# Three stages on one core: output tiles in threes, a later preparation, paired column groups and deferred routing

## The chip, the cores and the metric

The kernel runs on one core of a Trainium2 chip. The metric is the device time of one execution in microseconds (us), lower being better. Each time given for a kernel is the median of several runs. One further execution is taken with the hardware profiler; all rows of the trace come from it.

The core has a matrix engine (PE, with its weight loads shown as PEld), a vector engine (DVE), an engine for activations and copies (ACT, also called ScalarE), GpSimd (POOL) and a queue engine (SP) that issues most DMAs.

## What is computed

Three layers follow one another. The input of each is the output of the layer ahead of it.

```python
# attention: 4 batches x 8 heads, 576 positions, head_dim 64, 128 features
proj = q_or_k @ w_phi; proj -= max(abs(proj))
phi  = concat([exp(proj), exp(-proj)])
out  = (phi_q @ (phi_k.T @ v)) / (phi_q @ sum(phi_k) + 1e-6)
# routed experts: 2304 tokens, width 512, 8 experts, hidden width 1024
logits = x @ w_gate + modality_bias[modality_id]
e = argmax(logits);  g = softmax(logits)[e]
x = g * (relu(x @ w1[e]) @ w2[e])
# gated layer: hidden width 1536
out = ((x @ w_a) * (x @ w_b)) @ w_out
```

All inputs and the output are float32.

## The kernel before, in words

Products that have to be exact to about float32 are made of three matmuls (`mm3`, lines 51 to 54): each operand is split into a high and a low part, and high x high, high x low and low x high are added in PSUM. So every operand is first copied to its high part (mostly by ACT) and then has the low part made by a subtraction (mostly by DVE, in the attention partly by POOL).

**Order of the work.** The kernel is written in Tile: instructions are traced in program order, each gets a priority from its place in that order, and a list scheduler then lays down, from estimated durations, one fixed sequence for each engine; an engine runs its sequence strictly in order. `tc.high_priority(offset=-n)` makes what is traced inside it count as if it came n instructions later, so that it gives way to the next n. Only in the gated layer is the sequence of PE written by hand (`manual_schedule`, lines 866 and 870).

**Attention** (class `Attn`, lines 57 to 265) works in eight units of two heads and two batches, in nine rounds r (lines 912 to 921): in round r `a_steps(r)` makes the features of unit r (`phi`, `turn`) and its sums over positions (`kv`), `b_steps(r - 1)` finishes the unit before (`kvx`, lines 210 to 222, then `num`, lines 224 to 265), and `t_steps(r + 1)` splits the inputs of the next. `kvx` multiplies the sums by the gate weights and copies the product from PSUM to SBUF (tile `kx`, line 221, on DVE); `num` needs `kx`. `num` also leaves partial router logits in `lgp`.

**Routing** (class `Route`, lines 350 to 515) turns the logits of one half of the tokens (1152) into expert tiles: four steps, `start` (constants, gate), `rank`, `place` and `table`, each a chain of small DVE instructions with a few small matmuls. The steps of half 0 are put among the attention steps: `start` and `rank` in round 5, `place` in round 6, `table` in round 7 (line 921). Those of half 1 stand in the expert layer, at steps 0, 2, 4 and 6 (`side`, line 948).

**Experts** (class `Moe`, lines 518 to 650) run four tiles of up to 608 tokens, two for each half. A tile has eight steps (`NJ`), so there are 32 in all; k counts them. Steps 0 to 3 of a tile do two hidden blocks each (`l1`, lines 577 to 591), steps 4 to 7 one output block each (`l2`, lines 593 to 601). Both treat the 608 columns as two groups g of 304 (`CG`). In `l1` each group has a PSUM tile of its own out of six (`ps_l`, line 924); ACT takes the relu of it (tile `hh`, line 588) and DVE makes the low part (`hl`, line 589). In `l2` each group has a PSUM tile too, copied to `y` by ACT (line 601). Weights of a step are loaded two steps ahead and split (`splitw`, lines 545 to 552), tokens are gathered by POOL's indirect DMA (`gather`), transposed on PE and split (`transp`, lines 562 to 575, tiles `mxh` and `mxl`).

**Preparation** (`Moe2.prep`, lines 699 to 717, with `narrow`, lines 677 to 697) turns the weights of the gated layer, which come as 64-bit words, into float32, forms the sums that a Strassen-like scheme needs, splits them and stores them to DRAM (`wsc`). There are twelve blocks f; eight (`NPRE`) are prepared during the experts, spread evenly from step K0 = 0 to K1 = 27 of the 32 at a priority 200 lower (lines 951 to 957), four in the gated layer. At step K1 the buffers of the preparation are given back and the first weights and terms of the gated layer are fetched (`open_first`).

**Gated layer** (class `Moe2`, lines 653 to 872) runs 36 stages: three groups p of six output tiles (128 tokens x 512 each), twelve blocks f for each group. A stage makes seven products (`abp`, in two PSUM buffers, copied by ACT to `pc`, line 836), combines them on DVE, and adds the stage's part to the six accumulators of the group with the stage after it (`outp`, lines 802 to 813). After the last block of a group `finish` (lines 784 to 800) scales the six accumulators into SBUF tiles `o`, every other one on ACT (line 793) and DVE (line 791), and POOL scatters each to its rows of the output by an indirect DMA (line 794). The pool of `o` has `OB` = 2 buffers (line 674), so the third `o` waits until the first scatter has landed.

Of the kernel before, what the change touches and what calls it, by code (L numbers as in the profile page):

```python
# [20 lines left out]
P = 128  # L21
# [17 lines left out]
LOWP = 200  # L39
OB = 2  # L40
LOWP2 = 60
# [5 lines left out]
def f32(ap):  # L47
    return ap.bitcast(F32)
# [8 lines left out]
class Attn:  # L57
# [152 lines left out]
    def kvx(self, u, b):  # L210
        nc, st = self.nc, self.u[u]
        hp = u % 4
        ps = self.ps_t.tile([P, 512], F32, tag="t", name="kxp")
        t = st.pop(("kvs", b))
        for h in range(2):
            for c in range(2):
                i = 2 * h + c
                nc.tensor.matmul(ps[:, 73 * i:73 * i + 73], t[:65, 128 * i:128 * i + 128],
                                 self.cst["iw"][:, 2 * hp + h, :], start=True, stop=True)
        x = self.p_kx.tile([P, 4, 73], F32, tag=f"kx{b}", name="kx")  # L220
        nc.vector.tensor_copy(x, ps[:, :292].rearrange("p (i n) -> p i n", i=4))
        st["kx", b] = x
# [295 lines left out]
class Moe:  # L518
# [58 lines left out]
    def l1(self, T, f):  # L577
        nc = self.nc
        wh, wl = T["w", f // 2]
        for g in range(2):  # L580
            gs = slice(g * CG, g * CG + CG)
            ps = self.ps_l.tile([P, 512], F32, tag="l", name="hp")
            for c in range(4):
                i = 4 * (f % 2) + c
                mm3(nc, ps[:, :CG], wh[:, i, :], wl[:, i, :], T["xh"][:, c, gs], T["xl"][:, c, gs], c == 0, c == 3)
            hh = self.p_h.tile([P, CG], F32R, tag=f"h{f}{g}", name="hh")
            hl = self.p_h.tile([P, CG], F32R, tag=f"l{f}{g}", name="hl")
            nc.scalar.activation(hh, ps[:, :CG], AF.Relu)
            nc.vector.scalar_tensor_tensor(out=hl, in0=ps[:, :CG], scalar=0.0, in1=f32(hh), op0=ALU.max,
                                           op1=ALU.subtract)  # L590
            T["h", f, g] = (hh, hl)

    def l2(self, T, m):
        nc = self.nc
        wh, wl = T["w", 4 + m]
        for g in range(2):
            ps = self.ps_l.tile([P, 512], F32, tag="l", name="yp")
            for f in range(8):
                hh, hl = T["h", f, g]
                mm3(nc, ps[:, :CG], wh[:, f, :], wl[:, f, :], hh, hl, f == 0, f == 7)  # L600
            nc.scalar.copy(self.y[T["rt"].bp][:, m, ds(T["s"][g], CG)], ps[:, :CG])

# [50 lines left out]
class Moe2:  # L653
# [13 lines left out]
    def pools(self, ctx, ps_a, ps_l):  # L667
        tc = self.tc
        pool = lambda n, b: ctx.enter_context(tc.tile_pool(name=n, bufs=b, side="right", reuse_waits="tile"))
        self.p_w[1] = pool("f_w1", 1)  # L670
        self.p_t[1] = pool("f_t1", 4)
        self.p_c = pool("f_c", 1)
        self.p_g = pool("f_g", 2)
        self.p_o = pool("f_o", OB)
        self.ps_a, self.ps_l = ps_a, ps_l
# [103 lines left out]
    def run(self, ws, ts, src0, side):  # L779
# [4 lines left out]
        def finish(p):  # L784
            for m, acc in enumerate(accs.pop(p)):
                bp, b = divmod(2 * p + m // 3, HALF // n)
                o = self.p_o.tile([P, DM], F32, tag="o", name="o")
                c = b * (n // P) + m % 3
# [3 lines left out]
                else:  # L792
# [3 lines left out]
                    out_offset=bass.IndirectOffsetOnAxis(ap=self.routes[bp].perm[:, c:c + 1], axis=0),  # L796
                    in_=o[:, :], in_offset=None)
                for other in self.stores:
# [74 lines left out]


def interleave(*lists):
    items = []
    for n, l in enumerate(lists):
        for i, s in enumerate(l):
            items.append(((i + 0.5) / len(l), n, s))
    items.sort(key=lambda a: (a[0], a[1]))  # L880
    for _, _, s in items:
        s()
# [3 lines left out]
def trn_kernel(ctx, tc, qk, v, w_phi, mod_id, w_gate, bias, wm, wf, out):  # L886
# [10 lines left out]
    with ExitStack() as actx:  # L897
# [14 lines left out]
        for r in range(9):  # L912
            if r + 1 < 8:
                at.load(r + 1)
            if r == 2:
                bs = bias_sel(nc, cpool, keep, bias, mod_id)
                routes = [Route(nc, rpool, lgp[i], bs[i], i) for i in range(2)]
                rsteps = routes[0].steps(wkpool, at.ps_t)
            interleave(at.b_steps(r - 1) if r > 0 else [], at.a_steps(r) if r < 8 else [],
                       at.t_steps(r + 1) if r + 1 < 8 else [],  # L920
                       {5: rsteps[0:2], 6: rsteps[2:3], 7: rsteps[3:4]}.get(r, []) if r > 2 else [])
    with ExitStack() as mctx:
        ps_t = mctx.enter_context(tc.tile_pool(name="ps_t", bufs=2, space=PSUM, **tl))
        ps_l = mctx.enter_context(tc.tile_pool(name="ps_l", bufs=6, space=PSUM, **tl))
        ypool = ctx.enter_context(tc.tile_pool(name="y", bufs=1, **tl))
# [21 lines left out]
        rs = routes[1].steps(wk1, ps_t)  # L947
        side = {2 * f: [rs[f]] for f in range(4)}
        side[7] = [close_work]
# [4 lines left out]

        K0, K1 = 0, len(tiles) * mo.NJ - 5
        for f in range(NPRE):
# [27 lines left out]
    ps_l = ctx.enter_context(tc.tile_pool(name="ps_l2", bufs=2, space=PSUM, **tl))  # L984
    m2.pools(ctx, ps_a, ps_l)
    m2.run(ws, ts, src0[0], side)

# [56 lines left out]
```

## Time and profile before

| | us |
|---|---|
| median of 3 runs | 934.85 |
| the runs | 929.9, 934.85, 939.41 |
| the profiled execution | 940.45 |
| its span, first to last instruction | 938.7 |

A row of the timeline gives the start and the length of an instruction in us, what it does (engine, line, operation, output<-inputs, shape), and in brackets how long its engine sat idle before it and what ended the idle time. A window gives busy us of each engine in a stretch, then the TensorE clock that was granted there as a share of its higher level (1.00 is 2.4 GHz, 0.50 is 1.2 GHz; a value between them is a stretch that holds both). A group of lines gives the number of instructions, their busy time together and the mean length of one in ns.

### The profile page before, as it was taken

What the parts mean: (1) busy time and instruction counts of PE and PEld (TensorE: products, weight loads), DVE (VectorE), ACT (ScalarE), POOL (GpSimd) and SP (SyncE); (2) the same over time, 40 slices, a digit from 0 to 9 for tenths busy, and PEclk for the clock granted to TensorE, in tenths of its full rate; (3) what the DMA queues carried; (4) which work ended last, traced back from release to release, by engine and by line L of the source; (5) the groups of instructions that cost most, each with busy time, mean ns of one, the idle gap of its engine ahead of it and who ended that gap; (6) DMA issues with size and microseconds to landing.
All of it is one profiled execution on the core that took longest, in us unless ns stands there. A gap on an engine that the chain in (4) does not pass through costs nothing. (4 is left out here: it accounts for less than half of the span.)

```text
span 938.7 us, 15310 instructions
## 1 busy us (share of the span) xinstructions
PE 880.0 (94%) x5645; PEld 833.4 (89%) x5645; DVE 671.3 (72%) x1252; ACT 438.3 (47%) x806; POOL 187.4 (20%) x171
## 2 busy tenths in 40 slices
PE   6899999899799799999989999978999998999994
PEld 4899998899799799999988989967999998999993
DVE  7878899969799998986239889856454466554552
ACT  5577666555344454554324445444333344333332
POOL 6443333301343543220002111002000001000002
PEclk7999998899899799999989999979999999999998
DMA  7332330112567688795037998586666667766631
GB/s 246 102 104 77 105 105 13 29 57 64 199 203 268 245 287 307 277 322 188 29 131 290 371 317 312 189 305 206 213 202 205 203 201 244 223 203 202 202 124 67
DMA packets 74309, 179.21 MB, mean 191 GB/s; under 512 B 8912, under 2 KB 27808, under 8 KB 74224
## 3 DMA queue, kind: packets, MB, share of 16 engines
q1 hardware_dynamic: 71184, 168.39, 53.3%
q0 software_dynamic: 3040, 9.75, 3.1%
q8 instruction: 46, 0.75, 0.3%
q14 instruction: 39, 0.32, 0.1%
HBM read 140.36 MB, written 37.75 MB: 190 GB/s over the span
## 5 line engine op out<-in xcount | busy, mean ns | idle before, releaser
L836 ACT COPY pc<-abp 128x384 f32<-128x384 f32 x252 | 120.4, 479 | 195.6 <-PE abp L54 193.9
L52 PE MATMUL abp<-yh,fw 128*128 128x384 f32 x504 | 173.6, 344 | 16.1 <-DMA fw<-wsc 6.4
L54 PE MATMUL abp<-yh,fw 128*128 128x384 f32 x504 | 172.6, 342 | 0.2 <-DMA fw<-wsc 0.2
L53 PE MATMUL abp<-yl,fw 128*128 128x384 f32 x504 | 172.4, 342 | 0.0
L52 PEld LDWEIGHTS abp<-yh,fw 128*128 128x128 f32 x504 | 97.0, 192 | 25.9 <-ACT pc L836 7.6
L689 POOL TENSOR_SCALAR cvs<-cvs 128x768 f32<-128x768 f32 x24 | 59.2, 2468 | 250.4 <-ACT cvs L688 244.9
L53 PEld LDWEIGHTS abp<-yl,fw 128*128 128x128 f32 x504 | 97.0, 192 | 7.8
L54 PEld LDWEIGHTS abp<-yh,fw 128*128 128x128 f32 x504 | 96.7, 192 | 0.7 <-DMA fw<-wsc 0.7
L54 PE MATMUL op<-fw,gl 128*128 128x512 f32 x216 | 85.9, 398 | 1.3 <-DVE gl L826 1.3
L52 PE MATMUL op<-fw,gh 128*128 128x512 f32 x216 | 86.1, 398 | 1.0 <-ACT gh L825 1.0
L53 PE MATMUL op<-fw,gh 128*128 128x512 f32 x216 | 85.4, 395 | 0.0
L794 POOL DMA_INDIRECT out<-o,perm x18 | 17.7, 983 | 318.5 <-ACT o L793 311.7
L53 PE MATMUL hp<-mxl,wh 128*128 128x304 f32 x256 | 79.1, 310 | 1.5 <-DVE mxl L575 1.5
L52 PE MATMUL hp<-mxh,wh 128*128 128x304 f32 x256 | 79.5, 314 | 0.6 <-ACT mxh L574 0.6
L54 PE MATMUL hp<-mxh,wl 128*128 128x304 f32 x256 | 78.7, 308 | 0.0
L53 PE MATMUL yp<-hl,wh 128*128 128x304 f32 x256 | 77.3, 303 | 0.0
L52 PE MATMUL yp<-hh,wh 128*128 128x304 f32 x256 | 77.0, 303 | 0.0
L54 PE MATMUL yp<-hh,wl 128*128 128x304 f32 x256 | 77.0, 302 | 0.0
L236 PE MATMUL nmp<-kx,qts 128*128 128x73 f32 (+1 forms) x640 | 73.3, 271 | 1.8 <-DVE grest L478 1.8
L236 PEld LDWEIGHTS nmp<-kx,qts 128*128 128x128 f32 (+1 forms) x640 | 69.7, 187 | 4.0 <-issue 3.0
L185 ACT ACTIVATE qts<-qtp 128x512 f32<-128x512 f32 (+1 forms) x80 | 40.2, 552 | 47.0 <-PE qtp L182 46.8
L127 POOL TENSOR_TENSOR xtl<-qk,xth 128x512 fp32r<-128x512 f32 (+1 forms) x35 | 44.3, 1268 | 88.0 <-ACT xth L126 83.0
(201 smaller groups left out, 2052.9 us busy)
## 6 DMA issues: line engine op xcount, KB each, us to landing
fw<-wsc SPq DMA_DIRECT2D x72, 512.0 KB
fw<-wsc SPq DMA_DIRECT2D x144, 256.0 KB
raw<-in_moe_w SPq DMA_DIRECT2D x24, 768.0 KB
s<-in_moe_w SPq DMA_DIRECT2D x32, 512.0 KB
fw<-wsc SPq DMA_DIRECT2D x72, 128.0 KB
wsc<-whi SPq DMA_DIRECT2D x12, 640.0 KB
wsc<-wsum SPq DMA_DIRECT2D x12, 640.0 KB
wsc<-whi SPq DMA_DIRECT2D x12, 512.0 KB
```

The costliest lines, as they stand in the source:

```text
L52: nc.tensor.matmul(out, lh, rh, start=start, stop=False)
L53: nc.tensor.matmul(out, lh, rl, start=False, stop=False)
L54: nc.tensor.matmul(out, ll, rh, start=False, stop=stop)
L127: (nc.vector if u == 0 else nc.gpsimd).tensor_sub(lo[:, x:y], src, f32(hi[:, x:y]))
L185: nc.scalar.activation(t[:, s, :n, :], ps[:, :n, :], AF.Exp, scale=1.0 - 2.0 * s)
L236: nc.tensor.matmul(ps[pp, o, :], qt[:, c, a, pp], st["kx", b][:, 2 * h + c, :], start=c == 0, stop=c == 1)
L689: nc.gpsimd.tensor_scalar(out=s.bitcast(F32), in0=s.bitcast(F32), scalar1=LEAST, scalar2=None, op0=ALU.max)
L794: st = nc.gpsimd.indirect_dma_start(out=self.out[:, :], out_offset=bass.IndirectOffsetOnAxis(ap=self.routes[bp].perm[:, c:c + 1], axis=0), ...
L836: nc.scalar.copy(x, ps)
```

## The change

- `kvx` copies `kx` on ACT instead of DVE (line 221).
- `l1` puts both column groups into one PSUM tile of two banks and takes one relu and one low part over both (608 columns); `l2` takes one such tile for both groups, but still copies each by itself. The pool `ps_l` has three of these tiles instead of six of one bank.
- The pool of `o` is gone. `finish` takes its output tiles three at a time from the tag `raw` of the buffers that the gated layer's own preparation uses (`cv[1]`): two buffers of three tiles, so all six have a place.
- The routing steps of both halves, and the selection of the bias in round 2, are traced at a priority 80 lower (`LOWR`). Half 0 has `start`, `rank` and `place` in round 5 and `table` in round 6.
- The eight preparations are spread from step 3 to step 28 instead of 0 to 27, and `open_first` moves to step 28.

```diff
--- before.py
+++ after.py
@@ -37,7 +37,7 @@
 TB = 6
 NPRE = 8
 LOWP = 200
-OB = 2
+LOWR = 80
 LOWP2 = 60
 NWARM = 9
 NATIVE = (0,)
@@ -218,7 +218,7 @@
                 nc.tensor.matmul(ps[:, 73 * i:73 * i + 73], t[:65, 128 * i:128 * i + 128],
                                  self.cst["iw"][:, 2 * hp + h, :], start=True, stop=True)
         x = self.p_kx.tile([P, 4, 73], F32, tag=f"kx{b}", name="kx")
-        nc.vector.tensor_copy(x, ps[:, :292].rearrange("p (i n) -> p i n", i=4))
+        nc.scalar.copy(x, ps[:, :292].rearrange("p (i n) -> p i n", i=4))
         st["kx", b] = x
 
     def num(self, u, g):
@@ -577,28 +577,28 @@
     def l1(self, T, f):
         nc = self.nc
         wh, wl = T["w", f // 2]
+        ps = self.ps_l.tile([P, 2, 512], F32, tag="l", name="hp")
         for g in range(2):
             gs = slice(g * CG, g * CG + CG)
-            ps = self.ps_l.tile([P, 512], F32, tag="l", name="hp")
             for c in range(4):
                 i = 4 * (f % 2) + c
-                mm3(nc, ps[:, :CG], wh[:, i, :], wl[:, i, :], T["xh"][:, c, gs], T["xl"][:, c, gs], c == 0, c == 3)
-            hh = self.p_h.tile([P, CG], F32R, tag=f"h{f}{g}", name="hh")
-            hl = self.p_h.tile([P, CG], F32R, tag=f"l{f}{g}", name="hl")
-            nc.scalar.activation(hh, ps[:, :CG], AF.Relu)
-            nc.vector.scalar_tensor_tensor(out=hl, in0=ps[:, :CG], scalar=0.0, in1=f32(hh), op0=ALU.max,
-                                           op1=ALU.subtract)
-            T["h", f, g] = (hh, hl)
+                mm3(nc, ps[:, g, :CG], wh[:, i, :], wl[:, i, :], T["xh"][:, c, gs], T["xl"][:, c, gs], c == 0, c == 3)
+        hh = self.p_h.tile([P, 2, CG], F32R, tag=f"h{f}", name="hh")
+        hl = self.p_h.tile([P, 2, CG], F32R, tag=f"l{f}", name="hl")
+        nc.scalar.activation(hh, ps[:, :, :CG], AF.Relu)
+        nc.vector.scalar_tensor_tensor(out=hl, in0=ps[:, :, :CG], scalar=0.0, in1=f32(hh), op0=ALU.max,
+                                       op1=ALU.subtract)
+        T["h", f] = (hh, hl)
 
     def l2(self, T, m):
         nc = self.nc
         wh, wl = T["w", 4 + m]
+        ps = self.ps_l.tile([P, 2, 512], F32, tag="l", name="yp")
         for g in range(2):
-            ps = self.ps_l.tile([P, 512], F32, tag="l", name="yp")
             for f in range(8):
-                hh, hl = T["h", f, g]
-                mm3(nc, ps[:, :CG], wh[:, f, :], wl[:, f, :], hh, hl, f == 0, f == 7)
-            nc.scalar.copy(self.y[T["rt"].bp][:, m, ds(T["s"][g], CG)], ps[:, :CG])
+                hh, hl = T["h", f]
+                mm3(nc, ps[:, g, :CG], wh[:, f, :], wl[:, f, :], hh[:, g, :], hl[:, g, :], f == 0, f == 7)
+            nc.scalar.copy(self.y[T["rt"].bp][:, m, ds(T["s"][g], CG)], ps[:, g, :CG])
 
     def run(self, tiles, side={}):
         NT, NJ = len(tiles), self.NJ
@@ -671,7 +671,6 @@
         self.p_t[1] = pool("f_t1", 4)
         self.p_c = pool("f_c", 1)
         self.p_g = pool("f_g", 2)
-        self.p_o = pool("f_o", OB)
         self.ps_a, self.ps_l = ps_a, ps_l
 
     def narrow(self, pool, f, half, dst, nt):
@@ -784,7 +783,9 @@
         def finish(p):
             for m, acc in enumerate(accs.pop(p)):
                 bp, b = divmod(2 * p + m // 3, HALF // n)
-                o = self.p_o.tile([P, DM], F32, tag="o", name="o")
+                if m % 3 == 0:
+                    os = self.p_o.tile([P, 3, DM], F32, tag="raw", name="o", bufs=2)
+                o = os[:, m % 3, :]
                 c = b * (n // P) + m % 3
                 g2 = self.routes[bp].g2[:, c:c + 1]
                 if m % 2:
@@ -794,7 +795,7 @@
                 st = nc.gpsimd.indirect_dma_start(
                     out=self.out[:, :],
                     out_offset=bass.IndirectOffsetOnAxis(ap=self.routes[bp].perm[:, c:c + 1], axis=0),
-                    in_=o[:, :], in_offset=None)
+                    in_=o, in_offset=None)
                 for other in self.stores:
                     self.tc.declare_no_dep(st.ins, other, reason="each row of the output is stored once")
                 self.stores.append(st.ins)
@@ -870,6 +871,14 @@
         with self.tc.manual_schedule(engines={mybir.EngineType.PE}):
             for m in range(6):
                 outp(len(seq) - 1, m)
+
+
+def low(tc, step):
+    def run():
+        with tc.high_priority(offset=-LOWR):
+            step()
+
+    return run
 
 
 def interleave(*lists):
@@ -913,15 +922,16 @@
             if r + 1 < 8:
                 at.load(r + 1)
             if r == 2:
-                bs = bias_sel(nc, cpool, keep, bias, mod_id)
+                with tc.high_priority(offset=-LOWR):
+                    bs = bias_sel(nc, cpool, keep, bias, mod_id)
                 routes = [Route(nc, rpool, lgp[i], bs[i], i) for i in range(2)]
-                rsteps = routes[0].steps(wkpool, at.ps_t)
+                rsteps = [low(tc, st) for st in routes[0].steps(wkpool, at.ps_t)]
             interleave(at.b_steps(r - 1) if r > 0 else [], at.a_steps(r) if r < 8 else [],
                        at.t_steps(r + 1) if r + 1 < 8 else [],
-                       {5: rsteps[0:2], 6: rsteps[2:3], 7: rsteps[3:4]}.get(r, []) if r > 2 else [])
+                       {5: rsteps[0:3], 6: rsteps[3:4]}.get(r, []) if r > 2 else [])
     with ExitStack() as mctx:
         ps_t = mctx.enter_context(tc.tile_pool(name="ps_t", bufs=2, space=PSUM, **tl))
-        ps_l = mctx.enter_context(tc.tile_pool(name="ps_l", bufs=6, space=PSUM, **tl))
+        ps_l = mctx.enter_context(tc.tile_pool(name="ps_l", bufs=3, space=PSUM, **tl))
         ypool = ctx.enter_context(tc.tile_pool(name="y", bufs=1, **tl))
         y = [ypool.tile([P, 4, YC], F32, name=f"y{i}") for i in range(2)]
         m2 = Moe2(nc, tc, wf, wsc, y, routes, out, f64)
@@ -945,14 +955,14 @@
 
         wk1 = rctx.enter_context(tc.tile_pool(name="rwork1", bufs=1, **tl))
         rs = routes[1].steps(wk1, ps_t)
-        side = {2 * f: [rs[f]] for f in range(4)}
+        side = {2 * f: [low(tc, rs[f])] for f in range(4)}
         side[7] = [close_work]
 
         def conv(f):
             with tc.high_priority(offset=-LOWP):
                 m2.prep(f, cv[0], 2, 2)
 
-        K0, K1 = 0, len(tiles) * mo.NJ - 5
+        K0, K1 = 3, len(tiles) * mo.NJ - 4
         for f in range(NPRE):
             side.setdefault(K0 + (K1 - K0) * f // NPRE, []).append(lambda f=f: conv(f))
         ts, src0 = {}, []
@@ -983,6 +993,7 @@
     ps_a = ctx.enter_context(tc.tile_pool(name="ps_a2", bufs=1, space=PSUM, **tl))
     ps_l = ctx.enter_context(tc.tile_pool(name="ps_l2", bufs=2, space=PSUM, **tl))
     m2.pools(ctx, ps_a, ps_l)
+    m2.p_o = cv[1]
     m2.run(ws, ts, src0[0], side)
```

## Rows read from the trace of the kernel before

**Rows 1.** The page, part 1 (busy us, instructions), and the clock of the core
```profile
PE 880.0 (94%) x5645; PEld 833.4 (89%) x5645; DVE 671.3 (72%) x1252; ACT 438.3 (47%) x806; POOL 187.4 (20%) x171
...
core 0: 938.7 us, clock 0.957
```

**Rows 2.** Windows: length, busy us of PE, PEld, DVE, ACT, POOL, clock, DMA share, GB/s
```profile
148.00:157.00 9.00, 8.85 (x56) 8.66 (x57) 7.79 (x19) 4.66 (x10) 1.28 (x1) 0.62 0.10 31
...
179.00:190.00 11.00, 9.97 (x48) 9.73 (x49) 10.19 (x32) 7.88 (x14) 2.40 (x2) 0.53 0.37 107
...
275.00:300.00 25.00, 25.00 (x184) 25.00 (x184) 25.00 (x52) 11.63 (x18) 13.53 (x6) 1.00 0.75 254
...
312.00:321.00 9.00, 8.37 (x39) 8.07 (x40) 7.13 (x17) 2.48 (x4) 2.89 (x2) 0.59 0.99 362
...
619.00:628.00 9.00, 8.04 (x27) 7.44 (x28) 3.06 (x4) 3.63 (x6) 0.00 (x0) 0.58 0.89 321
...
654.00:658.00 4.00, 3.94 (x13) 3.72 (x14) 2.25 (x4) 0.86 (x3) 1.84 (x2) 0.60 0.43 84
...
797.00:802.00 5.00, 4.67 (x17) 4.38 (x18) 2.25 (x4) 1.19 (x4) 1.93 (x2) 0.66 0.38 73
```

**Rows 3.** Timeline of PE (start, us, what, idle before and its releaser)
```profile
148.15 1.09 PE L236 MATMUL nmp<-kx,qts 128*128 128x73 f32 x6 [1.81 <-DVE grest L478]
...
177.24 0.36 PE L52 MATMUL pjp<-wph,xth 128*128 128x256 f32 x1 [1.72 <-DVE rec L245]
...
179.88 0.45 PE L52 MATMUL kvp<-kh,vh 128*66 128x256 f32 x1 [1.69 <-ACT kh L167]
...
306.87 0.40 PE L495 MATMUL tbq<-tbqr,lhs 128*128 128x45 bf16 x9 [1.06 <-DVE top L942]
...
312.06 0.90 PE L571 MATMUL mxt<-ident,xg 96*128 96x96 f32 x4 [4.32 <-DVE mxl L575]
...
619.74 0.66 PE L52 MATMUL abp<-yh,fw 128*128 128x384 f32 x1 [6.37 <-DMA fw<-wsc]
...
654.06 0.69 PE L52 MATMUL abp<-yh,fw 128*128 128x384 f32 x1 [2.91 <-ACT pc L836]
...
797.34 0.69 PE L52 MATMUL abp<-yh,fw 128*128 128x384 f32 x1 [2.42 <-ACT pc L836]
```

**Rows 4.** Timeline of ACT and POOL at two finishes of output tiles
```profile
652.95 0.69 ACT L793 ACTIVATE o<-op,g 128x512 f32<-128x512 f32 x1 [2.23 <-DMA out<-o,perm]
...
925.61 0.97 POOL L794 DMA_INDIRECT out<-o,perm  x1 [0.30 <-issue]
...
933.39 0.97 POOL L794 DMA_INDIRECT out<-o,perm  x1 [0.45 <-DVE o L791]
```

**Rows 5.** Timeline of POOL and DVE in the fifth attention unit
```profile
143.61 2.71 POOL L113 TENSOR_TENSOR vl<-v,vh 128x1280 fp32r<-128x1280 f32 x1
...
143.73 2.63 DVE L478 TENSOR_TENSOR grest<-grest,gp 128x9 f32<-128x9 f32 x1
...
147.92 0.15 DVE L478 TENSOR_TENSOR grest<-grest,gp 128x9 f32<-128x9 f32 x1
```

**Rows 6.** Groups by line and shape (busy us, mean ns; idle before): attention, then experts
```profile
L221 DVE COPY kx<-kxp 128x292 f32<-128x292 f32 x16 | 7.3, 456 | 7.3 <-PE kxp L218 7.2
...
L551 DVE TENSOR_TENSOR wl<-s,wh 128x1024 fp32r<-128x1024 f32 x29 | 35.6, 1229 | 15.7 <-ACT wh L550 15.7
...
L589 DVE SCALAR_TENSOR_TENSOR hl<-hp,hh 128x304 fp32r<-128x304 f32 x64 | 29.3, 467 | 10.9 <-ACT hh L588 10.9
...
L550 ACT CAST wh<-s 128x1024 fp32r<-128x1024 f32 x29 | 30.4, 1050 | 21.3 <-PE yp L53 11.3 <-PE hp L53 8.8 <-DMA s<-in_moe_w 1.0
...
L588 ACT ACTIVATE hh<-hp 128x304 fp32r<-128x304 f32 x63 | 25.5, 423 | 22.6 <-PE hp L54 22.5
```

**Rows 7.** Window of the last expert tile, and the last preparation before it
```profile
425.00:481.00 56.00, 56.00 (x403) 55.79 (x402) 18.44 (x27) 17.90 (x33) 0.00 (x0) 1.00 0.25 81
...
418.32 1.49 DVE L715 TENSOR_TENSOR wsum<-wsum,whi 128x1280 fp32r<-128x1280 f32 x1 [1.71 <-ACT whi L714]
```

## Prediction

> **What bounds the kernel now.** I read the page first: PE is busy 94% of the span, and the mean granted clock is 0.957 [rows 1]. So the kernel can gain in two ways only: by filling PE's gaps (938.7 - 880.0 = 58.7 us), and by the stretches in which the clock is at its lower level. Then I read PE's timeline for the gaps and what ended them [rows 3], and for each the window behind it [rows 2]. The reader is to see that they go together: behind each gap of [rows 3] but the one at 306.87, which runs on into the next, PE works in a window whose granted clock is 0.53 to 0.66, while windows without a gap stand at 1.00. A gap is therefore paid twice. I price the second part as length of the window x (1 - clock), which counts the window's few idle tenths too:
> - 146 to 148: 1.81 + 9 x 0.38 = 5.2 us
> - 175 to 180: 1.72 + 1.69 + 11 x 0.47 = 8.6 us
> - 306 to 312: 1.06 + 4.32 + 9 x 0.41 = 9.1 us
> - 613 to 620: 6.37 + 9 x 0.42 = 10.2 us
> - 651 to 654: 2.91 + 4 x 0.40 = 4.5 us
> - 795 to 797: 2.42 + 5 x 0.34 = 4.1 us
>
> These six make 41.7 us. The sum is made against the profiled execution: 940.45 us, of which 1.75 lie around the span. It stands 5.6 us above the median of 934.85, so at the end I take the saving off the median. The gap at 613 waits for weights that the preparation in the gated layer stored late; no line of that part is changed, and I leave its 10.2 us where they are.
>
> **Six output tiles.** At the end of each group of stages ACT waits for a scatter to land before it may write the third or fifth output tile: 2.23 us at 652.95 [rows 4]. Because ACT is in order, the copy of `pc` queues behind that, and PE, whose two PSUM buffers are then full, waits for ACT, in the last two of [rows 3]. With a place for all six tiles no eviction waits for a scatter: the transfer that used `raw` before is the preparation's, whose last weights PE is already using at 619.74, so the place is free. Removed: 4.5 + 4.1 = 8.6 us. What is late next: up to two further evictions may now run ahead of a `pc` copy, 2 x 0.69 us [rows 4], at each of the two finishes; PE has two buffers ahead, so I take half, 0.7 us each, 1.4 together (bounds 0 and 2.8).
>
> At the very end six scatters follow one another. POOL issues them 0.97 + 0.30 = 1.27 us apart when it waits for nothing [rows 4]. The one at 925.61 is the second; four more would stand at 925.61 + 4 x 1.27 = 930.7 instead of 933.39. Saved 2.7 us (bounds 0, if the landings follow one another in any case, and 2.7). This part: 8.6 - 1.4 + 2.7 = 9.9 us.
>
> **Routing of half 0, and `kx` on ACT.** The two gaps at 146 and 175 are DVE's: it is busy 10.19 of 11 us in the second window [rows 2], and its small routing instructions stand among those that PE waits for. The `kx` copies leave it: 16 x 0.456 = 7.3 us [rows 6]. On ACT, the nearest row is the relu from PSUM over 304 columns, 0.423 us [rows 6], so 16 x 0.42 = 6.7 us. ACT is busy 4.66 of 9 and 7.88 of 11 us in those windows [rows 2], so its idle time hides them; uncovered, a copy would wait behind one cast of 1.05 us [rows 6] and `num` behind it, up to 16 x 1.05 = 17 us over the attention. I take 0, since the order of ACT is planned with the copy in it. The routing instructions stay, all of them; 80 places of low priority move them behind what is ready in the attention, while `place` and `table` are traced a round earlier. The selection of the bias goes back by 80 places too, with its nine loads on SP; its result is first used by `start` three rounds later, so I give it 0. No queue but DVE's holds up PE by this: their matmuls are few, and the constants on POOL and the loads on SP depend on nothing of PE. The gain lies between both gaps gone, 13.8 us, and the same gap once more, -8.6. I take half of the first, 6.9 us: the load on DVE falls by 7.3 us spread over 200, so the rows speak for fewer gaps, not for none.
>
> What the row shows of the first gap is not priority: a DVE instruction on nine columns, 0.15 us at 147.92, takes 2.63 us at 143.73, and ends with a POOL subtraction that began at 143.61 and took 2.71 [rows 5]. The Trainium skill (SBUF — State Buffer, section "SBUF: two separate sides") says that VectorE and GpSimd share a port pair as an exclusive lock that is held for the whole instruction, against a VectorE instruction with two SBUF inputs too. The trace agrees here. By that rule a lower priority only chooses which subtraction of POOL the routing meets, and this part would bring nothing instead of 6.9 us.
>
> **The experts: routing of half 1, and preparation from step 3.** From 275 to 300 us DVE is busy 25.00 of 25 [rows 2], with routing, preparation and the splits together; the gap at 306 to 312 is PE waiting for a split of tokens (`mxl`) in that queue. An expert tile lasts 56 us when nothing stalls [rows 7], a step 7, so the preparations' priorities move by 21 us at the start, and 7 at the end. With them go what each issues: two raw loads and four stores on SP, and two POOL instructions ahead of the gathers in that queue. For the routing, 80 places are about one and a half steps (403 PE instructions in eight steps [rows 7], 50 each), 11 us. The third tile needs that table: its tokens are transposed from four steps before it begins, 312 + 56 - 28 = 340, against a table whose last matmuls start at 306.87; the 33 us between hide the delay. The later preparation is hidden by the last tile: the last split ends at 419.8, and PE works at full clock without a gap until 481 [rows 7]. So 61 us hide a delay of 21, and the weights and terms that `open_first` fetches behind it. If that cover were gone the gated layer would start late by the excess. The 9.1 us lie between gone and still there; I take all of it, since the window at 275 is the only full one ahead of a gap and the change takes work out of just this stretch.
>
> **Paired groups.** 64 pairs of relu and low part become 32. From 304 to 1024 columns ACT's instruction grows from 0.423 to 1.050 us and DVE's from 0.467 to 1.229 [rows 6], so 608 columns cost 0.69 and 0.79: 0.16 and 0.14 us saved a pair, 5 us on each engine, none on PE's path. The cost: layer 2 needs the last hidden block after 21 matmuls of 56 / 403 = 0.139 us, 2.9 us; relu and low part take 1.5 from the end of the pair. If DVE is in the middle of a preparation's split, 1.49 us [rows 7], that makes 3.0. Before, the first group was split while the second was multiplied. I take 0.25 us for each of four tiles, 1.0 together (bounds 0 and 4 x 1.5 = 6).
>
> **Another order.** The list scheduler lays out the attention and the experts anew, and its durations know nothing of [rows 5]. I count one new gap, at the price of the one at 175, 8.6 us (bounds 0 and two of them).
>
> **Sum.** 9.9 + 6.9 + 9.1 - 1.0 - 8.6 = 16.3 us: the profiled execution would take 924.2, and the median 934.85 - 16.3 = 918.5.
>
> **Rivals.**
> - *Everything planned goes and nothing new comes*: 9.9 + 13.8 + 9.1 - 1.0 = 31.8, so 903. For it: each named gap has its engine relieved. Against it: the order is not written by hand. Chance 0.14.
> - *Routing meets POOL elsewhere*: the attention's gaps come back at other places. For it: [rows 5], whose long instruction is POOL's doing and not DVE's load. Against it: some of these collisions need not fall where PE is short. 16.3 - 6.9 = 9.4 saved, 925.5. Chance 0.16.
> - *Only the output tiles do what they say*: the low priorities move the gaps of attention and experts about, and `raw` gives the rest. 9.9 - 1.0 saved, less one new gap or none: 926 to 934.5. Chance 0.17.
> - *The pairs turn DVE's backlog into PE's wait*: slower. In the first three tiles DVE is near full; six single buffers let a low part be late by five groups (5 x 12 x 0.139 = 8.3 us), three pairs by two pairs (2 x 24 x 0.139 = 6.7), and the last block by 2.9 - 1.5 = 1.4 only. It decides once DVE is behind by more than 1.4 us at the end of layer 1 in each of these tiles; at 312 it was behind by 4.32 [rows 3]. Price: a gap like that one in three tiles, 3 x 9.1 = 27.3, so 918.5 + 27.3 = 945.8. Against it: DVE gets 5 us back and the planner gives the low part precedence over preparation. Chance 0.08.
>
> **How the numbers follow.** The forecast has the remaining 0.45. 1% is 9.3 us, about what a measurement of this kernel can tell from no change: faster is under 925.5, slower over 944.2. Faster: 0.45 + 0.14 + half of the second rival 0.08, and 0.03 of the third: 0.70. Slower: 0.08 and 0.02 for gaps of the third: 0.10. The rest, 0.20, is within 1%. The range goes from 900, just under the first rival, to 936, over the third; it leaves out the fourth and the ends of the others.
>
> **What would show it.** Right: no wait of ACT for `out` at the finishes and a last scatter about 4.5 us behind the last matmul; no PE gap over 2 us near 306 and at most one in the fifth to seventh unit; mean clock near 0.97; PE's gaps about 45 us. The boundary of layers 1 and 2 shows PE waiting for `hl` under 0.5 us. Wrong: PE waiting for `hh` or `hl` in three tiles, long small DVE instructions beside POOL's ahead of new gaps, or the gap at 613 gone or grown, which I left as it is.

## The result, and the profile after

The changed kernel takes 924.99 us (median of 20 runs), the kernel before 936.78 (20 runs beside them): ratio 0.9869 [0.9848, 0.9889], 11.8 us saved by the medians. The forecast was 16.3. The ratio leaves out one of the 20 runs, of 933.52 us, which was in a slower state; by the ratio the saving is 12.3.

The page's first part and the core's clock, of the kernel after (busy us, share of the span, instructions):

```profile
PE 877.7 (95%) x5645; PEld 828.1 (90%) x5645; DVE 658.7 (71%) x1204; ACT 438.3 (47%) x790; POOL 183.1 (20%) x171
...
core 0: 924.4 us, clock 0.971
```

Against [rows 1] the span is 14.3 us shorter in these two executions. PE's idle time went from 58.7 to 924.4 - 877.7 = 46.7 us, the mean clock from 0.957 to 0.971. ACT is as busy as before: the `kx` copies came to it (16 of 0.410 us by the groups, estimated 0.42), and the 32 paired relus gave back about as much (0.673 us each, estimated 0.69; the low part on DVE 0.783, estimated 0.79).

The timeline of PE, of the kernel after (start, us, what, idle before and its releaser), answers to [rows 3]:

```profile
167.27 0.66 PE L182 MATMUL qtp<-ident,df 128*128 128x128 f32 x4 [1.57 <-DVE df L152]
...
306.80 0.41 PE L52 MATMUL hp<-mxh,wh 128*128 128x304 f32 x1 [3.38 <-ACT y L601]
...
321.27 0.38 PE L52 MATMUL hp<-mxh,wh 128*128 128x304 f32 x1 [1.59 <-DVE hl L589]
...
374.94 0.41 PE L52 MATMUL hp<-mxh,wh 128*128 128x304 f32 x1 [1.94 <-DVE hl L589]
...
382.36 0.38 PE L52 MATMUL hp<-mxh,wh 128*128 128x304 f32 x1 [1.40 <-DVE hl L589]
...
617.86 0.66 PE L52 MATMUL abp<-yh,fw 128*128 128x384 f32 x1 [5.90 <-DMA fw<-wsc]
```

Five things are to be seen. The three gaps of the attention became one of that size, at another place. The gap of 4.32 us at 312 is gone, but the experts have new ones, 3.38 at 306 and three more for `hl`. The gap at 617 is the one at 613 of before, about as large as it was. And the two behind the output tiles, near 651 and 795, have no line any more: PE works at full clock through both finishes (the first evictions stand at 636.80 and 775.97), as the last two windows show. The windows (length, busy us of PE, PEld, DVE, ACT, POOL, clock, DMA share, GB/s) answer to [rows 2]:

```profile
168.00:185.00 17.00, 16.29 (x82) 15.49 (x80) 15.42 (x39) 7.71 (x13) 2.54 (x2) 0.51 0.27 80
307.00:312.00 5.00, 5.00 (x27) 4.97 (x27) 5.00 (x11) 0.13 (x1) 1.00 (x1) 0.66 0.93 296
375.00:382.00 7.00, 5.96 (x32) 5.72 (x32) 6.26 (x8) 2.42 (x4) 1.91 (x2) 0.76 0.78 252
384.00:390.00 6.00, 5.87 (x42) 5.65 (x42) 5.25 (x8) 3.35 (x5) 3.70 (x2) 1.00 0.95 294
618.00:626.00 8.00, 7.49 (x31) 6.72 (x32) 3.42 (x5) 4.05 (x7) 0.00 (x0) 0.74 0.89 318
636.00:656.00 20.00, 19.74 (x101) 18.24 (x102) 12.85 (x23) 8.87 (x18) 6.19 (x6) 1.00 0.80 272
776.00:796.00 20.00, 20.00 (x105) 18.51 (x104) 12.30 (x21) 8.68 (x18) 6.08 (x6) 1.00 0.83 286
```

Priced as in the prediction, the attention's one gap still costs 1.57 + 17 x 0.49 = 9.9 us, against 13.8 for the three of before, and the one at 617 costs 5.9 + 8 x 0.26 = 8.0 us.

The end, in POOL's timeline of the kernel after, answers to the last two of [rows 4]:

```profile
912.79 0.97 POOL L795 DMA_INDIRECT out<-o,perm  x1 [126.40 <-ACT o L794]
914.07 0.97 POOL L795 DMA_INDIRECT out<-o,perm  x1 [0.30 <-issue]
...
919.16 0.97 POOL L795 DMA_INDIRECT out<-o,perm  x1 [0.30 <-issue]
```

The six scatters follow one another 1.27 us apart, as assumed. PE's last matmul ends at 914.91; the last scatter begins 4.25 us later, against 933.39 - 926.44 = 6.95 before: 2.7 saved.

PE's waits in the experts, 239 to 480 us of the kernel after (engine, line, releaser: us in total, times, longest):

```profile
PE hp L52 <- DVE hl L589: 5.6, 4, 1.9
PE hp L52 <- ACT y L601: 3.4, 1, 3.4
PE yp L52 <- ACT y L601: 0.9, 2, 0.7
```

A matmul into `hp` does not read `hl` or `y`. It waits for its PSUM tile, which the low part or the copy of an earlier group still reads. In the same view of before these lines are absent. Its first three are:

```profile
PE mxt L571 <- DMA xg<-xs,idx: 4.8, 3, 3.8
PE mxt L571 <- DVE mxl L575: 4.3, 1, 4.3
PE hp L53 <- DVE mxl L575: 1.5, 1, 1.5
```

The first of them is a wait that no term of the forecast names: at the start of the experts PE waits for gathered tokens, 0.74 us at 239.47 and 3.76 at 245.47, and the clock behind is low. The change has 0.69 us of it, at 237.90, and a full clock. The windows from 245 to 252, before and then after:

```profile
245.00:252.00 7.00, 6.53 (x31) 6.56 (x31) 3.36 (x13) 1.87 (x4) 1.90 (x2) 0.57 0.66 248
...
245.00:252.00 7.00, 6.83 (x57) 6.56 (x56) 6.04 (x23) 4.67 (x7) 4.61 (x2) 1.00 0.23 81
```

Priced as in the prediction, that was 0.74 + 3.76 + 7 x 0.43 = 7.5 us.

### The profile page after: what moved, and what is told of

It reads as the page before. It is cut to its first block, busy times and chain, and to the rows that moved or that the text cites. A ratio compares the mean times of both kernels' runs of the same rounds, so it can differ in the third digit from the quotient of the medians.

```text
span 924.4 us, 15265 instructions
## 1 busy us (share of the span) xinstructions
PE 877.7 (95%) x5645; PEld 828.1 (90%) x5645; DVE 658.7 (71%) x1204; ACT 438.3 (47%) x790; POOL 183.1 (20%) x171
## 5 line engine op out<-in xcount | busy, mean ns | idle before, releaser
L688 POOL TENSOR_SCALAR cvs<-cvs 128x768 f32<-128x768 f32 x24 | 56.0, 2335 | 234.5 <-ACT cvs L687 234.3
L150 DVE TENSOR_REDUCE m<-pjp 128x4 f32<-128x512 f32 x72 | 48.7, 683 | 18.4 <-PE pjp L54 17.9
```

What stands on the lines that cost most here:

```text
L150: nc.vector.tensor_reduce(out=m, in_=pv, op=ALU.max, axis=AX.X, apply_absolute_value=True)
L688: nc.gpsimd.tensor_scalar(out=s.bitcast(F32), in0=s.bitcast(F32), scalar1=LEAST, scalar2=None, op0=ALU.max)
```

## The experiments

Ratios are against the kernel before, run on the same chip. How far single profiles can be compared showed only with e8: the kernel after, e2 and e8 issue the same instructions in the same order up to the gated layer, yet the first matmul into `hp` starts at 239.2, 235.9 and 245.0 us, and their experts end at 479.0, 473.4 and 479.1. A stage time of attention or experts from one profile is therefore good to some 6 to 9 us only, and the ratios decide.

**Output tiles, and each other part undone by itself.** e2 is the change without the output tiles (`OB = 2`, an own pool of single tiles), e5 the kernel before with the output tiles alone:

```diff
-                o = self.p_o.tile([P, DM], F32, tag="o", name="o")
+                if m % 3 == 0:
+                    os = self.p_o.tile([P, 3, DM], F32, tag="raw", name="o", bufs=2)
+                o = os[:, m % 3, :]
```

> The changed kernel with the two-buffer pool of output tiles back. Theory: the output tiles are most of the gain: both finish gaps come back (4.5 and 4.1 us with their clock) and the last scatter is 2.7 us later, so 11.3 us slower than the changed kernel, ratio to before 0.997 to 1.001. Rival: the output tiles gave only the end and the rest came from the layers ahead: 3 us slower, ratio 0.990.

> The kernel before with the output tiles alone (six places in the tag raw); nothing else changed. Theory: they are the whole gain, 9.8 us in the gated layer and 2.7 behind it: ratio to before 0.985 to 0.989. Rival: the other parts bring a third or more of the gain, so that this one alone gives 0.991 or more.

Measured: e2 0.9994 [0.9967, 1.0022], e5 0.9895 [0.9869, 0.9921]. The output tiles alone give 0.0105 x 936 = 9.8 us (forecast 9.9). Undone in the change they cost 0.0125 x 936 = 11.7 us, and without them the change gives nothing that can be measured. PE's timeline of e2 has the finish gaps again:

```profile
646.31 0.55 PE L53 MATMUL abp<-yh,fw 128*128 128x384 f32 x1 [2.18 <-ACT pc L837]
...
789.50 0.44 PE L53 MATMUL abp<-yh,fw 128*128 128x384 f32 x1 [2.10 <-ACT pc L837]
```

The gated layer, from its first to its last PE instruction, takes 441.7 us before and 441.5 in e2, against 431.9 after and 431.5 in e5.

e1 puts the single column groups back (`l1`, `l2` of before, six single PSUM tiles), e3 the routing, e4 the preparations' places:

```diff
-        ps_l = mctx.enter_context(tc.tile_pool(name="ps_l", bufs=3, space=PSUM, **tl))
+        ps_l = mctx.enter_context(tc.tile_pool(name="ps_l", bufs=6, space=PSUM, **tl))
...
-LOWR = 80
+LOWR = 0
-                       {5: rsteps[0:3], 6: rsteps[3:4]}.get(r, []) if r > 2 else [])
+                       {5: rsteps[0:2], 6: rsteps[2:3], 7: rsteps[3:4]}.get(r, []) if r > 2 else [])
...
-        K0, K1 = 3, len(tiles) * mo.NJ - 4
+        K0, K1 = 0, len(tiles) * mo.NJ - 5
```

> The changed kernel with the column groups single again (six one-bank PSUM tiles, 64 relus); all else as changed. Theory: the pairs cost time, because PE waits for a pair's low part or output copy before it may reuse one of three places; the profile after shows these waits (5.6 us for hl, 4.3 for the copies of y) and two low-clock stretches behind them worth 3.4. Without pairs they go: 5 to 10 us under the changed kernel, ratio to before 0.976 to 0.982. Rival: the pairs are neutral and the waits belong to DVE's backlog, which finds other waits: within 3 us of the changed kernel, ratio 0.984 to 0.990.

> The changed kernel with the routing at its plain priority and in its old rounds (start and rank in the fifth, place in the sixth, table in the seventh); kx stays on ScalarE. Theory: the place of the routing decides the attention's gaps, so those of before come back in the fifth and seventh unit: 5 to 9 us slower, ratio 0.992 to 0.997. Rival: what matters is where a small vector instruction meets a long one of GpSimd, which priority doesn't govern: within 3 us either way, ratio 0.984 to 0.990.

> The changed kernel with the eight preparations spread from step 0 to 27 again. Theory: the vector engine takes preparation whenever it has nothing else, so three steps of priority move little: within 3 us of the changed kernel, ratio 0.984 to 0.990. Rival, as in my forecast: the later start took the backlog at 306 us away, so its gap of 9.1 us with its clock comes back: ratio 0.994 to 0.999.

Measured: e1 0.9856 [0.9823, 0.9889], e3 0.9884 [0.9836, 0.9933], e4 0.9814 [0.9757, 0.9871]. None is clear of the change's own interval, so no gain of the pairs, the low priority or the later preparation on top of the rest is shown. In e3, with the routing back in its old place and `kx` on ACT, none of the attention's three gaps of before returns. In e1 the waits of `hp` for `hl` and `y` are gone, as they should be with six single tiles, but others stand in their place. PE's waits in the experts of e1:

```profile
PE mxt L571 <- DMA xg<-xs,idx: 5.7, 3, 3.4
PE rkp L392 <- DVE mx L383: 1.4, 1, 1.4
PE mxt L571 <- DVE mxl L575: 1.3, 1, 1.3
PE hp L52 <- ACT mxh L574: 1.1, 1, 1.1
```

And with the preparations early, in e4, no gap like the one at 312 of before comes back. PE's waits in the experts of e4:

```profile
PE yp L52 <- DVE hl L589: 3.0, 1, 3.0
PE hp L53 <- DVE mxl L575: 1.7, 1, 1.7
```

The first of these is the wait that I had looked for at the boundary of layers 1 and 2: 3.0 us, once, in this order.

**The `kx` copies.** e6 is the change with the copy on DVE again, e12 the kernel before with the copy on ACT and nothing else:

```diff
-        nc.vector.tensor_copy(x, ps[:, :292].rearrange("p (i n) -> p i n", i=4))
+        nc.scalar.copy(x, ps[:, :292].rearrange("p (i n) -> p i n", i=4))
```

> The changed kernel with the copies of kx back on the vector engine (7.3 us more there, 6.5 less on ScalarE). Theory: the attention's gaps are set by single long instructions and not by the vector engine's load, so within 3 us of the changed kernel: ratio 0.983 to 0.990. Rival: the load counts, and the gaps at 146 and 175 us of before come back, 5 to 14 us: ratio 0.992 or more.

> The kernel before with the copies of kx alone on ScalarE; routing, output tiles, groups and preparation as before. Theory: these copies, and not the priority of the routing, took away the gaps at 146 and 175 us (both came back with the copies on the vector engine): the gap of 1.8 us near 146 goes and the attention is 4 to 7 us shorter, ratio 0.992 to 0.996. Rival: it takes the low priority as well: ratio 0.997 or more.

Measured: e6 0.9923 [0.9895, 0.9952], e12 0.9897 [0.9855, 0.9940]. In PE's timeline of e6 the three gaps of [rows 3] return with the same releasers and lengths, although the routing has its low priority:

```profile
144.16 1.78 PE L236 MATMUL nmp<-kx,qts 128*128 128x73 f32 x14 [1.81 <-DVE grest L478]
...
171.66 0.36 PE L52 MATMUL pjp<-wph,xth 128*128 128x256 f32 x1 [1.72 <-DVE rec L245]
...
174.30 0.45 PE L52 MATMUL kvp<-kh,vh 128*66 128x256 f32 x1 [1.69 <-ACT kh L167]
```

So these gaps hang on the 16 copies, and not on the priority. e12, with the old priorities, does not have them: its timeline shows others, of 2.41 us at 166.79, 1.03 at 176.84 and 1.03 at 222.95. The last of them is PE waiting for a copy of `kx` on ACT, a wait that the forecast took as 0. The windows behind the first two and behind the last:

```profile
167.00:178.00 11.00, 9.96 (x52) 9.60 (x51) 10.30 (x30) 6.61 (x10) 3.08 (x2) 0.59 0.03 7
...
223.00:231.00 8.00, 8.00 (x43) 8.00 (x44) 3.15 (x11) 2.88 (x6) 0.53 (x1) 0.57 0.61 194
```

By the prediction's price these make 4.5 + 11 x 0.41 + 8 x 0.43 = 12.4 us, against 13.8 for the three of before. What e12 clearly lacks lies in the experts: it has no gap at 306, though its preparations stand where they stood in the program. PE's waits in its experts (238 to 462 us), and there is no more than this:

```profile
PE mxt L571 <- DMA xg<-xs,idx: 2.0, 1, 2.0
PE hp L52 <- ACT mxh L574: 0.7, 2, 0.5
```

while e5, whose order of attention and experts is that of before, has the gap of 4.32 us for `mxl` again, at 308.20. So the gap goes with one order, which the copies alone already change.

**POOL in pieces.** e7 is the change with POOL's copy `vh` in two instructions, its subtraction `vl` in four, and `xtl` in pieces of 256 columns:

```diff
-        nc.gpsimd.tensor_sub(vl[:, :, 0:64], st["v"], f32(vh[:, :, 0:64]))
+        for j in (0, 5, 10, 15):
+            nc.gpsimd.tensor_sub(vl[:, j:j + 5, 0:64], st["v"][:, j:j + 5, :], f32(vh[:, j:j + 5, 0:64]))
...
```

> The changed kernel with GpSimd's work of the attention from the second unit on in pieces: vl in four (0.7 us instead of 2.7), vh in two (0.65 instead of 1.25), xtl in pieces of 256 columns (0.73 instead of 1.27). The work stays. Theory: a small vector instruction waits for the GpSimd instruction beside it to end, so its wait falls to the length of a piece: the 19.6 us by which routing instructions of the attention are long fall under 12, the gap of 1.6 us at 167 and the low clock behind it go, and the attention is 3 to 8 us shorter, ratio 0.979 to 0.984. Rival: the vector engine meets the next piece again, the waits keep their sum, and the attention stays: ratio 0.984 to 0.990.

Measured: 0.9814 [0.9789, 0.9839], clear of the change's interval: some 5 us better, from an edit that adds instructions and removes no work. The timelines of POOL and DVE of the kernel after show what it cures:

```profile
163.34 2.68 POOL L113 TENSOR_TENSOR vl<-v,vh 128x1280 fp32r<-128x1280 f32 x1
...
164.06 0.21 DVE L417 TENSOR_REDUCE vals<-sel 128x9 f32<-128x72 f32 x1
164.19 1.85 DVE L431 SCALAR_TENSOR_TENSOR pl<-jbq,rc 128x9 f32<-128x9 f32 x1
165.96 0.16 DVE L440 SCALAR_TENSOR_TENSOR col<-col,jbq 128x9 f32<-128x9 f32 x1
...
166.54 0.68 DVE L152 TENSOR_TENSOR df<-pjp,m 128x512 f32<-128x512 f32 x1
```

An instruction on nine columns takes 1.85 us and ends with POOL's subtraction (163.34 + 2.68 = 166.02); `df` stands behind it, and PE waits for `df` at 167.27. I added up, over the attention, every DVE instruction of routing and bias that lasts more than 0.3 us longer than the shortest of its line. The excess is 20.7 us in 21 instructions before, 19.6 in 21 after (16 of each end within 0.25 us of the end of a POOL instruction), and 10.7 in 19 in e7. Some lines hold instructions of several shapes, of which the larger ones are long anyhow. With tiles and shapes kept apart it is 15.3 us in 15 before, 16.2 in 16 after and 7.4 in 14 in e7, and every one of these ends within 0.25 us of the end of a POOL instruction.

PE still has gaps there in e7, of 1.03, 0.82 and 0.89 us from 167 to 172, but the clock stays at its higher level, where it fell to 0.51 after:

```profile
165.00:185.00 20.00, 17.26 (x165) 16.23 (x165) 19.95 (x58) 13.23 (x23) 6.42 (x7) 1.00 0.28 85
```

And in all four kernels with the pieces (e7, e9, e10, e11) the first matmul into `hp` starts at 232.0 to 232.8 us, against 235.9 to 246.1 in the ten without. So a good part of the gain lies in the attention.

**The weights of the gated layer.** e8 places the four preparations of the gated layer one stage apart instead of two, e9 is e7 with a ninth preparation in the experts, and e10 and e11 take back the later preparation, and then the pairs too, on top of e9:

```diff
-        side.setdefault(2 * (f - NPRE), []).append(lambda f=f: m2.prep(f, cv[1], 1, 1))
+        side.setdefault(f - NPRE, []).append(lambda f=f: m2.prep(f, cv[1], 1, 1))
...
-NPRE = 8
+NPRE = 9
```

> The changed kernel with the last four preparations one stage apart instead of two in the gated layer. Theory: the gap at 612 (5.9 us, and 3.4 of clock behind it) is the last preparation's store coming late; traced three stages earlier it comes in time, and 6 to 9 us go: ratio 0.977 to 0.981. Rival: the preparations follow one another through single buffers as fast as the vector engine lets them, so the place in the program moves nothing: ratio 0.985 to 0.989.

> The changed kernel with GpSimd's work in pieces (as in the run before of that name) and nine preparations in the experts, three left for the gated layer. Theory: the gap at 612 is there because four preparations one behind the other take until 615 us, whatever their place in the program; three end some 28 us sooner, so the gap and its clock go, 8 to 10 us under the pieces alone (0.9814): ratio 0.970 to 0.974. Rival: the ninth preparation costs the experts as much in waits, or another load comes late: 0.978 or more.

> The same with the preparations spread from step 0 to 27 again. Theory: the later start brought nothing, and an earlier one leaves more room to nine preparations: 0 to 5 us under the kernel with nine preparations from step 3, ratio 0.966 to 0.972. Rival: the later start keeps the backlog of the vector engine out of the routing of half 1: 3 us or more slower than it, ratio 0.975 or more.

> The same (nine preparations from step 0, pieces) with the column groups single again. Theory: the pairs cost little beside their waits for hl, some 2 to 4 us: 2 to 4 us under the kernel with pairs, ratio lower by 0.002 to 0.004. Rival: pairs and single groups are alike: ratio within 0.002.

Measured: e8 0.9858 [0.9823, 0.9893], e9 0.9712 [0.9674, 0.9749], e10 0.9697 [0.9654, 0.9740], e11 0.9692 [0.9648, 0.9736]. In e8 no instruction and no DMA changes its place on any engine, so it is a second run of the same order, and says only that the place in the program is not what holds the late weights back. That four preparations behind one another in single buffers do is my reading; e9 tests their number. SP's timeline of the kernel after has, for the last of the four, the store of the first columns' high part and the load of the same columns:

```profile
606.21 0.38 SPq L715 DMA_DIRECT2D wsc<-whi  x1
...
612.80 0.32 SPq L725 DMA_DIRECT2D fw<-wsc  x1
```

SP waits for the store to land before it issues the load, the load lands 4.9 us after its issue, at 617.7, and PE's gap ends at 617.86. With one preparation fewer in the gated layer the gap is gone. PE's waits from 470 to 905 us, e7 first:

```profile
PE abp L52 <- DMA fw<-wsc: 5.7, 1, 5.7
PE abp L52 <- ACTq L991: 3.9, 1, 3.9
```

and e9:

```profile
PE abp L52 <- ACTq L991: 3.8, 1, 3.8
PE abp L52 <- ACT pc L843: 1.7, 4, 0.9
```

The gated layer goes from 431.7 us in e7 to 423.7 in e9. e9 to e11 cannot be told apart; each beats both kernels, e11 by its median of 907.09 us the most. So here too, no gain of the later preparation or of the pairs shows.

## Why the prediction came out as it did

**Output tiles: right, in mechanism and size.** Forecast 9.9, alone 9.8, undone 11.7. The tail gave the 2.7 of the sum. The 1.4 for evictions that run ahead of a `pc` copy, on the other hand, do not show: the longest gap near the finishes, 0.59 us at 636.26, waits for `gl` and stands ahead of the first eviction, and there is none from there to 656, or from 776 to 796.

**Routing and `kx`: a gain of this order, one of the two causes wrong.** The step that failed is "80 places of low priority move them behind what is ready in the attention". e6 has that priority and the three gaps; e12 and e3 lack it and have none of the three. The copies were the better half of the argument. Alone they are worth 0.0103 x 936 = 9.6 us, undone in the change (0.9923 - 0.9869) x 936 = 5.1, against 6.9 for both edits. But the 9.6 are not the term that was forecast: by the prices above e12's attention gains little, 13.8 to 12.4, and the gap at 312, which another term counts, goes with them. In the change itself the attention's price falls from 13.8 to 9.9, 3.9 of the 6.9. Whether the 7.3 us of load count or only the other order that the copies make, no run separates. (The reading that both gaps are DVE's was too simple also: the 1.69 us at 179.88 in [rows 3] are released by ACT's `kh`.)

What the copies did at the first gap can be read. In e6 the instruction on `grest` starts at 139.74 beside POOL's subtraction of 139.63 and takes 2.63 us, as in [rows 5]; after, the two instructions of this line stand at 141.01 and 141.93, with no POOL instruction beside the first, and take 0.16 and 0.17. They only stand elsewhere: the excess in the whole attention is nearly what it was (20.7 and 19.6 us), which speaks for the order, and the 1.57 us at 167.27 are a new meeting, with `pl`. That is the mechanism of the rival "routing meets POOL elsewhere". The rule of the Trainium skill (SBUF — State Buffer, section "SBUF: two separate sides"), an exclusive lock held for the whole instruction, agrees with it and with e7: with shorter instructions on POOL the excess falls to 10.7 us. The rival's price, nothing gained, was wrong, since the meetings come at places of different cost.

**The experts: wrong.** The step is "I take all of it, since the window at 275 is the only full one ahead of a gap and the change takes work out of just this stretch". The gap at 306 did go, but it goes without the later preparation too (e12, e4), and in its place stand the waits of 5.6, 3.4 and 0.9 us. Its stage is no shorter: from the first matmul into `hp` to the last into `yp` it takes 235.0 us before and 239.8 after, within what single profiles scatter. A full engine ahead of a gap was a sign of this order, not a cause that later preparation removes; DVE in e12 is busy 24.39 of 25 us in the same stretch, 266 to 291, with no gap behind it. What the change did lose at the start of the experts, the 7.5 us around the gather, was put at nothing: the forecast's list of gaps passed it over. Which edit takes it away stays open; e5, in the order of before, has 0.89 and 1.99 us of it, e12 1.95.

**Paired groups: the term "0.25 us for each of four tiles, 1.0 together" mis-sized, and its place too.** The profile after shows 5.6 us of waiting for `hl` and 4.3 for `y`, nearly all at tiles that `hp` wants back, where I had looked only at the boundary of the layers. Three double tiles come free half as often as six single ones. Yet e1 takes these waits away and gains nothing clear, since others take their place. The rival that made this 27.3 us slower asked for a gap in three tiles at the price of the one at 306; the waits after are there, but short. By the windows above the clock behind them is 0.66 for 5 us behind the first, 0.76 for 7 behind the third, and 1.00 behind the fourth, which costs 3.4 us, about the 3.7 behind 312 of before.

**Another order: the term of 8.6 us was there, but not as one gap.** `kx` alone and the output tiles alone would make 0.9897 x 0.9895 = 0.979 if they added up; the change has 0.9869. The other edits, beside these two, so would give back some 0.008 x 936 = 7 us. The comparison that shows such a loss without adding up is e2 against e12: pairs, low priority and later preparation on top of `kx` take 0.9897 [0.9855, 0.9940] to 0.9994 [0.9967, 1.0022]. Without `kx` on ACT they cost little: e6 0.9923 against e5 0.9895, with overlapping intervals. Which of the three it is stays open, as e1, e3 and e4 undo one at a time and none is clear; e4, with the lowest ratio, hints at the later preparation, and e10 against e9 does not repeat it.

**The gap at 613: right.** It stayed, with 6.37 before and 5.90 after, and e9 shows what it is worth: 0.9814 to 0.9712, some 9.5 us by the ratios and 8.0 in the gated layer, against a price of 10.2 for gap and low clock together.

In sum: 9.9 was right. If each part counts with what it gives alone, the 6.9 came out as some 9.6, from the copies and with part of the experts in it, and what the other edits and the new order were to give, 9.1 - 1.0 - 8.6 = -0.5, came out as 11.8 - 9.8 - 9.6 = -7.6. Counted so, that term, for an order which these rows could not tell, makes the forecast 4.5 us too good. Counted by what each part costs when undone, 11.7 and 5.1, the other edits give 11.8 - 11.7 - 5.1 = -5.0. That the total came so close is partly luck: the 9.1 rest on a reason that the runs do not bear out, the 8.6 against them were a guess, and the two nearly cancel. Of the signs of being wrong that the prediction lists, two are there, a long small DVE instruction beside POOL's ahead of the new gap at 167, and PE waiting for `hl` (though at `hp`'s tiles); and a gap over 2 us near 306 did appear.

## What to carry to other kernels

Price a gap of the matrix engine twice, by itself and by the low clock behind it, and count it as removable only if you can name the instruction that goes away: a gap in a list-scheduled stage belongs to that one order, and any edit, even 16 copies in the stage ahead, may remove or replace it. Where small VectorE instructions last ten times too long, look at GpSimd beside them and cut its instructions into pieces. Measure each part alone as well as undone, since parts need not add up: here two of them alone gave 0.990 each, and all together 0.987.

## What the runs showed that I had not expected

The same order of instructions did not give the same clock. The kernel after and e8 both have the gap of 1.56 or 1.57 us before `qtp`, at 167.27 and 168.24. Windows of the kernel after, just behind it:

```profile
168.00:172.00 4.00, 4.00 (x22) 4.00 (x21) 4.00 (x8) 1.55 (x3) 1.26 (x1) 0.52 0.03 8
172.00:185.00 13.00, 12.29 (x62) 11.49 (x61) 11.42 (x32) 6.16 (x10) 1.27 (x1) 0.50 0.34 102
```

and of e8:

```profile
166.00:170.00 4.00, 2.44 (x23) 2.29 (x21) 4.00 (x11) 1.07 (x3) 0.99 (x1) 1.00 0.06 16
170.00:183.00 13.00, 10.24 (x58) 9.49 (x57) 13.00 (x35) 5.83 (x11) 2.54 (x2) 0.63 0.17 38
```

After the gap the granted clock is at 0.5, the lower of its two levels (1.2 and 2.4 GHz), for all of the 17 us in the one, while in the other it stays at 1.00 at first and falls later, behind a second gap (2.24 us, 173.82) that the first kernel, slower by then, does not have. At 196 us the two stand within 0.3 us of each other again. They part behind a later gap, which both have too: PE waits 0.56 us for `kvs`, until 226.25 and 225.96. Behind it, in the kernel after and then in e8:

```profile
227.00:244.00 17.00, 14.76 (x130) 13.72 (x129) 10.75 (x38) 5.26 (x11) 4.01 (x5) 1.00 0.77 236
...
227.00:244.00 17.00, 16.85 (x84) 16.45 (x85) 6.91 (x26) 4.32 (x9) 2.62 (x3) 0.53 0.43 137
```

This is where e8 falls 6 us behind at the start of the experts. What decides which clock an execution gets, these runs do not show. The runs of the kernel after agree with the clock having a part in their spread: the shortest, 917.63 us, has a mean clock of 0.983, and one of 929.75 us has 0.966.
